# Moving weight loads behind output transposes in a fused attention and feed-forward kernel on Trainium2

## The chip, the cores and the metric

The kernel runs on one core of one Trainium2 chip. The metric is the device time of one execution in microseconds (us), as the median over several executions. In the profile, PE is TensorE (PEld its weight loads), DVE is VectorE, ACT is ScalarE, POOL is GpSimd and SP is SyncE. A q behind an engine's name means an instruction of its sequencer, such as one that issues a DMA. SP does no arithmetic here: it only issues DMAs and waits, strictly one after another.

## The reference

One transformer block with conditioning is computed for 2048 rows of width 1024, all in bf16:

```
mod = (silu(c) @ w_mod) in six rows:  sa, ca, ga, sb, cb, gb
h = layernorm(x) * (1 + ca) + sa
q = h @ wq                               # 32 heads of 128
k, v = the last 512 rows of the caches   # 4 key/value heads, each used by 8 query heads
o = softmax(q k^T / sqrt(128)) v
x = x + ga * (o @ wo)
h = layernorm(x) * (1 + cb) + sb
x = x + gb * ((silu(h @ w_gate) * (h @ w_up)) @ w_down)   # inner width 3584
```

## The kernel before, in words

**Tiling.** The rows are cut into 4 chunks of 512. One long loop (line 895) runs over `i`, one head of one chunk per iteration: 32 heads by 4 chunks are 128 heads. The loop is a software pipeline. In iteration `i` PE first projects the queries of head `i+3` (`qproj`: 8 matmuls of 512 columns, weights from a `wq` tile), then multiplies queries and keys of head `i-1` (`scores`: 4 matmuls of 512 columns, with the exponentials on ACT), then multiplies probabilities and values of head `i-2` (`pv`: 16 matmuls of 129 columns). After that DVE divides by the row sums (L824, L827), and SP issues a DMA transpose of the head's output into `oT_all` (L830). When the last head of a chunk is through `pv`, `oproj` multiplies all 32 turned heads by `wo`: 8 pieces of 32 matmuls, in the order of the heads. The last chunk's `oproj` is written out by hand behind the loop (lines 1005 to 1014), so that 44 matmuls on heads 0 to 27 come before the first that need heads 28 to 31. Then comes the feed-forward part, 28 tiles (`gateup`) and 8 pieces (`down`) for each chunk.

**Loads.** The query weights come in groups of four heads, 1 MB each (`load_wq`, L357), into slots that are used in turn. One is issued in every iteration with `i % 4 == 1`, for heads that `qproj` reaches four iterations later. Between iterations 34 and 85, 24 blocks of `w_mod` are loaded through a DMA transpose (`load_mt`, L582); these are the "turned weights", and DVE reduces each one four iterations after its load (`mod_col`, L587). The output weights `wo` (L840) and parts of x (L302) are loaded during the first iterations, and `ln_task` puts in DMA transposes for the next chunk's layer norm (L448). All of these are issued by SP in program order. The gate and up weights (`load_wgu`, L998 and L1000) are issued by ACT; the first two groups, four loads of 1 MB, stand directly behind the loop.

**Order.** Nothing is scheduled automatically. Each engine runs its instructions in the order in which the program emits them, and a small tracker puts in a wait where a buffer (`_Buf`) is read after a write, or written after a read. What the tracker knows of a buffer is its name, not its bytes: two pieces of one tile that share a `_Buf` wait for each other.

**The end.** `down` writes each finished piece with two DVE instructions of `resid` (L846 multiplies, L848 adds the residual and writes the tile `y_s`), and SP sends it to DRAM. The last 128 rows go out in three pieces of 512, 384 and 128 columns (L1071), from one tile `y_s[3]` under one `_Buf`, `B_y[3]`.

Of the kernel before, what the change touches and what calls it, by code (L numbers as in the profile page):

```python
# [7 lines left out]
P = 128  # L8
# [122 lines left out]
def bass_adaLN_cond__sliding_block_cached__swiglu_ffn__prompt_kernel(  # L131
# [17 lines left out]
    Hq = HD // Dh  # L149
# [111 lines left out]
    with nc.Block() as block:  # L261

        @block.gpsimd
        def _(g):
# [23 lines left out]
            def finish(gen):  # L288
                while gen in bg:
# [6 lines left out]
                 reads=[B_ident], writes=[B_ident])  # L296
# [50 lines left out]
            def wq_slot(gidx):  # L347
                return gidx if gidx <= NWQ else (gidx + 1) % NWQ
# [3 lines left out]
            def load_wq(gidx):  # L352
                if gidx >= NCH * HG:
                    return
                sl = wq_slot(gidx)
                hg = gidx % HG
                T.op(Q_wq[sl], lambda: SP.dma_start(  # L357
                    wq_s[sl], A_wq[:, hg * 512:(hg + 1) * 512].rearrange("(k p) n -> p k n", p=P)), writes=B_wq[sl])
# [139 lines left out]
            def mod_ca(hf, k):  # L498
# [6 lines left out]
                 reads=[B_cT, B_ident], writes=[PB[XB]])  # L505
# [7 lines left out]
                 reads=[B_x[tl]], writes=[B_ns4[tl], B_acc])  # L513
# [10 lines left out]
            def norm_last(c0, n):  # L524
# [9 lines left out]
                 reads=[B_acc], writes=[B_nm])  # L534
            T.op(ACT, lambda: A.activation(nsc4[tl], x_res[:, tl, :], AF.Square, bias=nmean[:, 0:1], accum_out=acc[:, 1:2]),
                 reads=[B_x[tl], B_nm], writes=[B_ns4[tl], B_acc])
# [41 lines left out]
            def load_mt(n):  # L578
                if n < 2:
                    for b_ in B_qT[NQT:]:  # L580
                        B_mt[n].absorb(b_)
                T.op(Q_mt[n % 2], lambda: SP.dma_start_transpose(  # L582
                    mt[n % 2].rearrange("p (a b) -> p a b", a=1), w_mod[:, (NF + n) * P:(NF + n + 1) * P]),
                     writes=[B_mt[n % 2]])
# [34 lines left out]
            B_oT = [_Buf("oT%d" % h) for h in range(Hq)]  # L619
# [224 lines left out]
            def resid(b, t, c0, n, ri, k, dst, dst_buf):  # L844
                s = k % 2
                T.op(DVE, lambda: V.tensor_tensor(tmp[s][:, 0:n], bank(b, n), rowb[ri][:, c0:c0 + n], ALU.mult),  # L846
                     reads=[B_row[ri]], writes=[PB[b], B_tmp[s]])
                T.op(DVE, lambda: V.tensor_tensor(dst[:, c0:c0 + n], tmp[s][:, 0:n], x_res[:, t, c0:c0 + n], ALU.add),  # L848
                     reads=[B_tmp[s], B_x[t]], writes=[dst_buf])
# [43 lines left out]
            LOADT = {Hq + 2 + (9 * n) // 4: n for n in range(NL)}  # L893
            LOADO = {5 + (21 * p) // 8: p for p in range(8)}
            for i in range(1, NA + 2):
                ch, h = divmod(i, Hq)
                if i % 4 == 1 and i > 5 or i == 4:
                    load_wq((i + 4) // 4 + 1)
                if 2 <= i < NQ0:
                    q_shifted(i)  # L900
                if i in (2, 3):
                    load_wga(i - 2)
                if i in LOADX:
                    load_x(LOADX[i])
                if i in LOADO:
                    load_wo(LOADO[i])
                if i in GATET:
                    gate_turn(GATET[i])
                if i in GATES:
                    gate_sum(GATES[i])  # L910
                if i in TURNT:
                    if i > Hq:
                        T.op(DVE, lambda: V.tensor_copy(mstg[:, 0:DT], mcol[:, 2 * DT:3 * DT]), reads=[B_mcol], writes=[B_mstg])
                    row_turn()
                if i in PUTT:
                    row_put(*PUTT[i])
                if i in GETT:
                    row_get(*GETT[i])
                if i == 7:
                    add_ln1(1)  # L920
                if h == 2 and 1 <= ch < NCH - 1:
                    add_ln1(ch + 1)
                if h == 2 and ch == NCH - 1:
                    add_ln2(0)
                if i + LEAD < NA:
                    if (i + LEAD) % Hq == 0:
                        finish(ln1[(i + LEAD) // Hq])
                    if i == 1:
                        scores(0)
                    if i in (1, 3, 5):  # L930
                        q_bias_mm(i + 1, i + 3, XB)
                    if i > NQ0:
                        qproj(i + LEAD)
                    elif i % 2 == 1:
                        qproj_mm(NQ0 + i // 2, QB, 0, HK)
                    else:
                        qproj(NQ0 - 1 + i // 2, QB, HK)
                if i - 4 in LOADT:
                    n = LOADT[i - 4]
                    mod_col(n)  # L940
                    g0, last = divmod(n, DT)
                    if last == DT - 1:
                        mod_take(g0, B_late[g0 + 1])
                        if g0 == 1:
                            mod_gain(1, B_late[2], B_g[1])
                if i in LOADT:
                    load_mt(LOADT[i])
                n = i - (NA - LEAD)
                if 0 <= n <= 2:
                    oproj_mm(NCH - 1, 0, QB, 8 * n, 8 * n + 8)  # L950
                elif n >= 3:
                    oproj_mm(NCH - 1, 1, XB, 8 * (n - 3), 8 * (n - 3) + 8)
                if 1 <= i - 1 < NA:
                    scores(i - 1)
                for gk in {2: (1,), 4: (2,), 6: (3,)}.get(i, ()):
                    k_turn(gk, XB)
                    kd, ks = k_evac(gk, XB)
                    T.op(DVE, lambda: V.tensor_copy(kd, ks), writes=[PB[XB], B_kT[gk]])
                    if gk == Hkv - 1:
                        for b_ in B_hT[1]:  # L960
                            for kb in B_kn:
                                b_.absorb(kb)
                if 0 <= i - 2 < NA:
                    pv(i - 2)
                    ch2, h2 = divmod(i - 2, Hq)
                    if h2 == Hq - 1 and ch2 < NCH - 1:
                        oproj(ch2)
                run_bg(1)
                for n in GATEP.get(i, ()):
                    gate_part(n)  # L970
                if i in GATER:
                    gate_row(GATER[i])
                if i == max(GATER):
                    gate_split()
# [10 lines left out]
            B_wg = [_Buf("wg%d" % i) for i in range(NWG)]  # L985
            B_wu = [_Buf("wu%d" % i) for i in range(NWG)]
            wg_s = [arena.at(OFF_G[i], [DT, 512], BF16, [B_wg[i]]) for i in range(2)]
# [2 lines left out]
            Q_wu = [dq("q_wu%d" % i, A) for i in range(NWG)]  # L990
            FG = FT // 4

            def load_wgu(G):
                if G >= NCH * FG:
                    return
                fg = G % FG
                sl = G % NWG
                T.op(Q_wg[sl], lambda: A.dma_start(  # L998
                    wg_s[sl], B_w_gate[:, fg * 512:(fg + 1) * 512].rearrange("(k p) n -> p k n", p=P)), writes=[B_wg[sl]])
                T.op(Q_wu[sl], lambda: A.dma_start(  # L1000
                    wu_s[sl], B_w_up[:, fg * 512:(fg + 1) * 512].rearrange("(k p) n -> p k n", p=P)), writes=[B_wu[sl]])

            load_wgu(0)
            load_wgu(1)
            HL = Hq - 4
            oproj_mm(NCH - 1, 1, XB, 16, HL)
# [16 lines left out]
            B_sg = [_Buf("sg%d" % i) for i in range(2)]  # L1023
            sg_s = [arena.at(OFF_SG + i * KB, [CH], BF16, [B_sg[i]]) for i in range(2)]
            B_y = [_Buf("y%d" % i) for i in range(4)]
            y_s = [arena.at(OFF_Y + i * 2 * KB, [D], BF16, [B_y[i]]) for i in range(4)]
            NWDP = 7
            B_wd = [_Buf("wd%d" % i) for i in range(NWDP)]
# [28 lines left out]
            def down(ch):  # L1057
                last = ch == NCH - 1
                pieces = [(j, hf * 512, 512) for j in range(TPC) for hf in range(2)]
                if last:  # L1060
                    pieces[-1:] = [(TPC - 1, 512, 384), (TPC - 1, 896, 128)]
                for k, (j, c0, n) in enumerate(pieces):
                    t = ch * TPC + j
                    b = 4 + k % 2
                    for ft in range(FT):
                        mm(bank(b, n), guT[:, ft, j * P:(j + 1) * P], wd_s[:, ft, c0:c0 + n],
                           ft == 0, ft == FT - 1, [B_wd[ft // (FT // NWDP)], B_gu[ft]], PB[b])
                    resid(b, t, c0, n, 1, k, y_s[t % 4], B_y[t % 4])
                    q = t % 4
                    if last and j == TPC - 1:  # L1070
                        T.op(Q_fin[k % 3], lambda: SP.dma_start(of[t * P:(t + 1) * P, c0:c0 + n], y_s[q][:, c0:c0 + n]),  # L1071
                             reads=[B_y[q]])
                    elif c0 == 512:
                        T.op(Q_out[q], lambda: SP.dma_start(of[t * P:(t + 1) * P, :], y_s[q]), reads=[B_y[q]])
                    run_bg(1)
# [48 lines left out]
```

## Time and profile before

| what | us |
|---|---|
| median of 3 runs | 1272.57 (1272.42 to 1273.69) |
| profiled execution, its own time | 1273.07 |
| its span, first to last instruction | 1271.1 |
| PE busy | 1264.0 (99%) |
| DVE busy | 485.8 (38%) |
| ACT busy | 341.6 (27%) |
| POOL busy | 55.9 (4%) |
| DMA queue of SP, share of the 16 DMA engines | 32.3% |
| DMA queue of ACT, share of the 16 DMA engines | 14.7% |

The first three rows say how the numbers stand to each other: the profiled execution took 2.0 us outside its span, and was itself 0.5 us above the median. The busy times are shares of the span; PE is busy almost throughout, at a granted clock of 1.00, and the other engines work beside it. The shares of the queues are averages over parts with very different loads.

### The profile page before, as it was taken

How to read it: one execution, taken by the hardware profiler on the slowest of the kernel's cores; microseconds unless marked ns; L12 is line 12 of the kernel's file. 1: busy time of each engine (PE TensorE's matmuls, PEld its weight loads, DVE VectorE, ACT ScalarE, POOL GpSimd, SP SyncE). 2: the span in 40 equal slices, each digit the busy share in tenths (PEclk: the TensorE clock that was granted, in tenths of full speed). 3: DMA queues.
4: the chain of work that ended last, by engine and by line, in shares of the span. 5: the costliest groups of instructions: out<-in, count | busy, mean ns of one | idle time of the engine just before them, and what ended most of it. 6: DMA issues, size and time to landing. Idle time of an engine off the chain costs nothing.

```text
span 1271.1 us, 17772 instructions
## 1 busy us (share of the span) xinstructions
PE 1264.0 (99%) x7595; PEld 641.9 (50%) x7595; DVE 485.8 (38%) x897; ACT 341.6 (27%) x389; POOL 55.9 (4%) x95
## 2 busy tenths in 40 slices
PE   9999999999999999999999999999999999999998
PEld 5655545555455554555544444444444444444444
DVE  4676226764257641365322321233212321221122
ACT  4655204553035550155510111011100111011100
POOL 1530000000000000000000000000000000000000
PEclk9999999999999999999999999999999999999999
DMA  9999405975028550066252973055512654044200
GB/s 314 283 257 218 91 1 117 206 147 121 1 62 175 129 136 16 9 133 142 38 145 100 290 240 100 25 157 150 166 42 72 176 141 133 17 132 150 67 9 25
DMA packets 238765, 156.67 MB, mean 123 GB/s; under 512 B 131680, under 2 KB 224608, under 8 KB 238688
## 3 DMA queue, kind: packets, MB, share of 16 engines
q1 hardware_dynamic: 180432, 96.83, 32.3%
q10 hardware_dynamic: 58256, 58.73, 14.7%
q8 instruction: 59, 0.97, 0.3%
q14 instruction: 18, 0.15, 0.0%
HBM read 120.33 MB, written 4.20 MB: 98 GB/s over the span
## 4 chain that ended last, share of the span: by engine, by line
PE 97%; DMA 2%; DVE 0%; SPq 0%; issue 0%; DVEq 0%
PE ps L271 97%; DMA arena<-arena 1%; DMA arena<-in_w_mod_dram 0%; PE ps L275 0%; SPq L309 0%; DMA out_dram<-arena 0%; DVE arena L827 0%; SPq L334 0%; DVE arena L587 0%; DVE arena L848 0%; DVE arena L490 0%; DVE arena L638 0%; DVE tmp L846 0%; SPq L582 0%; DVE rl L824 0%
## 5 line engine op out<-in xcount | busy, mean ns | idle before, releaser
L271 PE MATMUL ps<-arena 128*128 128x512 bf16 (+1 forms) x7354 | 1258.3, 334 | 3.5 <-POOL arena L298 2.0
L271 PEld LDWEIGHTS ps<-arena 128*128 128x128 bf16 x7354 | 633.4, 98 | 621.2 <-issue 2.2
L806 ACT ACTIVATE arena<-ps 128x1024 bf16<-128x1024 f32 x256 | 261.9, 1023 | 346.5 <-PE ps L271 334.8
L1053 ACT ACTIVATE arena<-ps 128x512 bf16<-128x512 f32 x112 | 66.9, 597 | 506.9 <-PE ps L271 506.9
L1054 DVE TENSOR_TENSOR arena<-ps,arena 128x512 bf16<-128x512 f32 x112 | 77.4, 691 | 276.3 <-PE ps L271 276.3
L846 DVE TENSOR_TENSOR tmp<-ps,rowb 128x512 f32<-128x512 f32 (+1 forms) x65 | 44.4, 683 | 319.9 <-PE ps L271 319.9
L638 DVE CAST arena<-ps 128x512 bf16<-128x512 f32 x120 | 82.8, 690 | 48.5 <-PE ps L271 48.5
L827 DVE TENSOR_TENSOR arena<-ps,rl 128x512 bf16<-128x512 f32 x128 | 88.5, 691 | 4.7 <-DVE rl L824 0.2
L824 DVE RECIPROCAL rl<-ps 128x4 f32<-128x4 f32 x128 | 23.3, 182 | 112.8 <-PE ps L271 112.8
L423 POOL TENSOR_SCALAR rstd<-mv 128x1 f32<-128x1 f32 x28 | 6.1, 216 | 912.5 <-DVE mv L422 912.5
L418 DVE BATCH_NORM_STATS2 st<-x_res 128x6 f32<-128x512 bf16 x62 | 42.3, 683 | 3.6 <-DMA x_res<-in_A_x_dram 3.5
L587 DVE SCALAR_TENSOR_TENSOR arena<-arena 128x1024 bf16<-128x1024 bf16 x24 | 29.1, 1214 | 0.0
L848 DVE TENSOR_TENSOR arena<-tmp,x_res 128x512 bf16<-128x512 f32 (+2 forms) x33 | 22.3, 676 | 2.1 <-DMA out_dram<-arena 1.0
L848 DVE TENSOR_TENSOR x_res<-tmp,x_res 128x512 bf16<-128x512 f32 x32 | 22.1, 692 | 1.1
L434 DVE TENSOR_SCALAR arena<-arena,gain,mod_bf 128x512 bf16<-128x512 bf16 x56 | 21.2, 420 | 0.0
L429 DVE TENSOR_SCALAR nsc<-x_res,mv,rstd 128x1024 bf16<-128x1024 bf16 x30 | 19.2, 641 | 0.0
L425 POOL TENSOR_TENSOR rstd<-rstd,mhalf 128x1 f32<-128x1 f32 x28 | 15.7, 559 | 2.3
L765 POOL TENSOR_SCALAR arena<-arena,sc_bf 128x512 f32<-128x512 bf16 x8 | 12.6, 1576 | 0.5 <-POOL arena L767 0.2
L767 POOL TENSOR_TENSOR arena<-arena 128x512 f32<-128x512 f32 x8 | 10.1, 1265 | 0.7
L422 DVE BATCH_NORM_AGGREGATE mv<-st 128x2 f32<-128x12 f32 x28 | 5.8, 209 | 1.0
L271 PEld LDWEIGHTS ps<-sc_bf,arena 128*128 128x128 bf16 x128 | 4.4, 96 | 1.8 <-DMA arena<-in_w_mod_dram 0.4
L271 PE MATMUL ps<-sc_bf,arena 128*128 128x1 bf16 x128 | 4.6, 164 | 0.2
(57 smaller groups left out, 62.6 us busy)
## 6 DMA issues: line engine op xcount, KB each, us to landing
arena<-in_A_wq_dram SPq DMA_DIRECT2D x31, 1024.0 KB, 5.9
arena<-in_B_w_gate_dram ACTq DMA_DIRECT2D x28, 1024.0 KB, 5.3
arena<-in_B_w_up_dram ACTq DMA_DIRECT2D x28, 1024.0 KB, 7.9
arena<-in_A_wo_dram SPq DMA_DIRECT2D x8, 1024.0 KB, 7.1
arena<-in_B_w_down_dram SPq DMA_DIRECT2D x7, 1024.0 KB, 8.0
out_dram<-arena SPq DMA_DIRECT2D x15, 256.0 KB, 2.0
x_res<-in_A_x_dram SPq DMA_DIRECT2D x3, 1024.0 KB, 6.7
arena<-arena SPq DMA_TRANSPOSE x132, 2.8
```

The lines of the kernel that those rows point to most:

```text
L271: T.op(PE, lambda: TE.matmul(out_ap, lhsT, rhs, start=start, stop=stop, skip_group_check=skip), reads=reads, writes=[bank_buf])
L418: T.op(DVE, lambda: V.bn_stats(st_[sl][:, hf * 6:hf * 6 + 6], x_res[:, t, hf * 512:hf * 512 + 512]), reads=[B_x[t]], writes=[B_st[sl]])
L434: T.op(DVE, lambda: V.tensor_scalar(dst[:, dt, :], dst[:, dt, :], gain[gi][:, dt:dt + 1], mod_bf[:, ccol + dt:ccol + dt + 1], op0=ALU.mult ...
L587: T.op(DVE, lambda: V.scalar_tensor_tensor(mt[n % 2], mt[n % 2], 1.0, sc_row, op0=ALU.mult, op1=ALU.mult, accum_out=mcol[:, n:n + 1]), rea ...
L638: T.op(DVE, lambda: V.tensor_copy(qT_s[qs], bank(b)), writes=[PB[b], B_qT[qs]])
L806: T.op(ACT, lambda: A.activation(ex_s[es][:, 2 * kp:2 * kp + 2, :], banks2(SCB + 2 * kp), AF.Exp, scale=att_scale), writes=[PB[SCB + 2 * k ...
L824: T.op(DVE, lambda: V.reciprocal(rl[r][:, :].rearrange("p (a b) -> p a b", a=2), psap(PVB * 512 + P, [[512, 2], [130, 2]])), writes=both + ...
L827: T.op(DVE, lambda: V.tensor_tensor(o_s[os_].rearrange("p (a b) d -> p a b d", a=2), psap(PVB * 512, [[512, 2], [130, 2], [1, P]]), rlb, A ...
L846: T.op(DVE, lambda: V.tensor_tensor(tmp[s][:, 0:n], bank(b, n), rowb[ri][:, c0:c0 + n], ALU.mult), reads=[B_row[ri]], writes=[PB[b], B_tmp ...
L848: T.op(DVE, lambda: V.tensor_tensor(dst[:, c0:c0 + n], tmp[s][:, 0:n], x_res[:, t, c0:c0 + n], ALU.add), reads=[B_tmp[s], B_x[t]], writes= ...
L1053: T.op(ACT, lambda: A.activation(sg_s[ss], bank(gb), AF.Silu), writes=[PB[gb], B_sg[ss]])
L1054: T.op(DVE, lambda: V.tensor_tensor(guT[:, ft, :], bank(ub), sg_s[ss], ALU.mult), reads=[B_sg[ss]], writes=[PB[ub], B_gu[ft]])
```

## The change

Three edits are made.

1. In the loop, `load_wq` (for all but iteration 4) and `load_mt` are emitted behind `pv(i - 2)`, and so behind the output transpose of head `i-2`, but before `oproj` where a chunk ends. They stood ahead of it: `load_wq` at the start of the iteration, `load_mt` after `qproj` and `mod_col`.
2. The first gate load behind the loop gets the turned outputs of heads 30 and 31 (`B_oT[30]`, `B_oT[31]`) as buffers that it reads. ACT therefore waits for those two transposes to land before it issues this load and the three behind it.
3. The last piece of the output, 128 columns, gets a buffer of its own, `B_yl`, in place of `B_y[3]`. The bytes stay where they were.

```
             for i in range(1, NA + 2):
                 ch, h = divmod(i, Hq)
-                if i % 4 == 1 and i > 5 or i == 4:
+                if i == 4:
                     load_wq((i + 4) // 4 + 1)
...
-                if i in LOADT:
-                    load_mt(LOADT[i])
...
                 if 0 <= i - 2 < NA:
                     pv(i - 2)
                     ch2, h2 = divmod(i - 2, Hq)
+                    if i % 4 == 1 and i > 5:
+                        load_wq((i + 4) // 4 + 1)
+                    if i in LOADT:
+                        load_mt(LOADT[i])
                     if h2 == Hq - 1 and ch2 < NCH - 1:
                         oproj(ch2)
...
-            def load_wgu(G):
+            def load_wgu(G, after=()):
...
                 T.op(Q_wg[sl], lambda: A.dma_start(
-                    wg_s[sl], B_w_gate[:, fg * 512:(fg + 1) * 512].rearrange("(k p) n -> p k n", p=P)), writes=[B_wg[sl]])
+                    wg_s[sl], B_w_gate[:, fg * 512:(fg + 1) * 512].rearrange("(k p) n -> p k n", p=P)),
+                     reads=list(after), writes=[B_wg[sl]])
...
-            load_wgu(0)
+            load_wgu(0, B_oT[Hq - 2:])
             load_wgu(1)
...
+            B_yl = _Buf("yl")
...
-                    resid(b, t, c0, n, 1, k, y_s[t % 4], B_y[t % 4])
                     q = t % 4
+                    yb = B_yl if last and k == len(pieces) - 1 else B_y[q]
+                    resid(b, t, c0, n, 1, k, y_s[q], yb)
                     if last and j == TPC - 1:
                         T.op(Q_fin[k % 3], lambda: SP.dma_start(of[t * P:(t + 1) * P, c0:c0 + n], y_s[q][:, c0:c0 + n]),
-                             reads=[B_y[q]])
+                             reads=[yb])
```

## The prediction

> **What bounds the kernel now.** I read the page first, then the waits, the chain that ended last, the timeline at the places that these name, and the groups by shape. From the page, busy time (share of the span, instructions) and the clock granted in the 40 slices:
>
> ```profile
> PE 1264.0 (99%) x7595; PEld 641.9 (50%) x7595; DVE 485.8 (38%) x897; ACT 341.6 (27%) x389; POOL 55.9 (4%) x95
> PEclk9999999999999999999999999999999999999999
> ```
>
> PE is idle for 1271.1 - 1264.0 = 7.1 us, and its clock is full throughout. No matmul is added or removed, so only these 7.1 us, and stalls that matmul records hide by overlapping, can change. The waits (us in total, times, longest) tell what they are:
>
> ```profile
> PE ps L271 <- POOL arena L298: 2.0, 1, 2.0
> PEld ps L271 <- DMA arena<-arena: 1.9, 3, 1.0
> DVE arena L848 <- DMA out_dram<-arena: 1.0, 1, 1.0
> PE ps L271 <- DMA arena<-arena: 0.7, 2, 0.5
> ```
>
> The first is the start, which the change leaves alone. The second and fourth are matmuls, and their weight loads, that wait for output transposes; the third is the last DVE instruction, behind a DMA. The chain that ended last (start, us, what) gives their places:
>
> ```profile
> 307.25 0.47 SPq L582
> ...
> 307.82 5.64 DMA arena<-arena
> ...
> 641.39 9.35 DMA arena<-arena
> ...
> 1266.73 0.57 DVE arena L848
> ...
> 1267.32 1.62 DMA out_dram<-arena
> ...
> 1269.04 0.29 DVE arena L848
> ```
>
> The timeline shows both PE stalls, and what SP did ahead of the first:
>
> ```profile
> 305.06 0.53 SPq L357 DMA_DIRECT2D arena<-in_A_wq_dram  x1
> 306.43 1.30 SPq L582 DMA_TRANSPOSE arena<-in_w_mod_dram  x1
> 307.82 1.48 SPq L830 DMA_TRANSPOSE arena<-arena  x1
> ...
> 313.51 2.76 PE L271 MATMUL ps<-arena 128*128 128x512 bf16 x12 [0.52 <-DMA arena<-arena]
> ...
> 650.79 19.38 PE L271 MATMUL ps<-arena 128*128 128x512 bf16 x89 [0.23 <-DMA arena<-arena]
> ```
>
> At 307.82 the transpose of a chunk's last head goes out behind a 1 MB load and a turned load, and `oproj` stops for it.
>
> **How long the stalls are.** The brackets count from the modelled end of the matmul before. Matmuls start every (19.38 - 0.38) / 88 = 0.216 us, but one lasts 0.379 us by the groups by shape; so a bracket leaves out 0.379 - 0.216 = 0.16 us. The stalls are 0.52 + 0.16 = 0.68 us and 0.23 + 0.16 = 0.39 us. Bounds are the brackets alone (0.75 together) and PEld's idle time at the same places (1.01 and 0.72).
>
> **Edit 1, what it gains.** DVE's L827 of that head ends at 307.25 in the chain, so the transpose can be issued there. Transposes land 2.4 us after issue at best and 2.7 in the median (min/median/max of L830: 2.4/2.7/9.8), here by 310.0; PE wants it at 313.51 - 0.68 = 312.8. That stall goes, 0.68 us. At the other two chunk ends inside the loop PE has no gap, only PEld one of 0.17 us, so nothing is gained there. Late next is nothing: the two loads that now follow serve heads behind 55 us of `oproj`.
>
> **Edit 1, what it costs.** The 28 query loads from iteration 9 on move behind one more output transpose each, and with it behind DVE's L827 of that head. In a quiet stretch (SP's rows, then DVE's cast of the first head that uses this load):
>
> ```profile
> 570.11 0.53 SPq L357 DMA_DIRECT2D arena<-in_A_wq_dram  x1
> 572.32 1.19 SPq L830 DMA_TRANSPOSE arena<-arena  x1
> ...
> 583.60 0.69 DVE L638 CAST arena<-ps 128x512 bf16<-128x512 f32 x1 [0.82 <-PE ps L271]
> ```
>
> The landing of all L357 loads, from the line's own view:
>
> ```profile
> DMA to landing us min/median/max: 5.4/5.9/10.6
> ```
>
> The load goes out at 572.32 + 1.19 = 573.5, 3.4 us later. PE starts on it 8 x 0.216 + 0.2 us ahead of the cast, at 581.7. So 8.2 us are left for a landing of 5.9: 2.3 to spare, no stall. The tight places are in the first chunk, where `wo` and x share the queue. The load at 95.96 took 9.2 us, to 105.2, and is wanted at 107.5 (cast at 109.40). Moved, it lands between 0.5 us later (in a full queue it only changes places with a small transpose) and 3.4 later: from 1.8 to spare to 1.1 late. The load at 70.13 took 7.5, to 77.6, wanted at 79.5 (cast at 81.43); the next transpose was issued 0.6 us behind it, so its shift is 1.2 (one transpose's issue) to 2.8: from 0.7 to spare to 0.9 late. After these the worst landing is 7.2 us at 543.49, which keeps 0.9. So edit 1's cost is 0 to 2.0 us. I take 0: the queue holds the same work in another order, which is the first end of each pair.
>
> [...]
>
> The 24 turned loads go out about 3.4 us later too. The shortest time from such an issue to the DVE reduction that reads it (L587) is 231.7 - 219.6 = 12.1 us, the longest landing 6.7, so 2.0 are left. The first one, at 141.36, is now queued behind the next chunk's first transpose (198.88), lands by 206.8 at the latest, and is read at 210.8. If one were late, DVE would hold up its cast and so PE. L448, L840 and L302 are queued on SP behind the moved instructions as before, only up to 3 us later; none has a waiter that near.
>
> **Edit 2.** The last two transposes were issued at 638.76 and 641.39 and took 9.8 and 9.3 us, while four 1 MB loads from ACT (637.62 to 640.26) were in flight; without these, by 2.4 to 2.7 us, they land by 644.1. PE wants them at 650.4: the stall of 0.39 goes. Behind ACT's new wait are the four loads, a table load of 1.28 us, and then nothing until the first L1053 at 689.20. The loads landed 17.5 us after the first issue (640.26 + 14.8); from 644.1 that is 661.6, and PE wants the first at 689.20 - 16 x 0.216 = 685.7. With 24 us of cover the wait costs nothing.
>
> **Edit 3.** The last L848 could start when its L846 ends, 1267.70 + 0.29 = 1267.99, and starts at 1269.04. With its own buffer it starts at 1268.02, a gain of 1.02. The final DMA then goes out at about 1268.34 with the piece before still in flight; its landing of 1.4 us may become 1.7 as for the first of the three pieces. So the gain is 0.7 to 1.0; I take 1.02, since DMAs of 96 and 32 KB leave the engines nearly empty.
>
> **The sum.** 0.68 + 0.39 + 1.02 = 2.09 us off the span: 1269.0. With the 2.0 us outside, the profiled execution would be 1271.0 against 1273.07. That execution lies 0.5 above the median, so the median becomes 1272.57 - 2.09 = 1270.5 us. A measurement of this kernel can tell about 0.2% from no change, 2.55 us; the forecast, 0.16%, is inside that.
>
> **Rivals.**
> *Only the end is gained (0.13).* The stalls hang on how DMAs fall, and the profiled execution is 0.5 us above the median; ordinary runs may have less of them. The third edit alone gives 1272.57 - 1.02 = 1271.5. It includes the case that the last two DMAs get in each other's way, and that one or two query loads are late (1272.57 - 2.09 + 2.0 = 1272.5).
> *Longer stalls than shown (0.18).* The slowest of the three runs is 1.1 us above the median, so some runs hold more than this profile. By PEld's idle times the gain is 1.01 + 0.72 + 1.04 = 2.77: 1269.8, faster by more than 0.2%. Against it: the matmul starts show 1.07 for the two, and the median run is the shorter one.
> *Query weights arrive late (0.07), slower.* The place is `qproj` at the start of every fourth iteration. It decides from a landing of 8.2 us, which the profile shows passed only at the start and in the crowded first chunk; to pass +0.2% it must cost 2.09 + 2.55 = 4.64 us, 0.17 us for each of 28 loads. At a mean landing of 8.5 us it would be 28 x 0.3 = 8.4 us: 1278.9. Against it: the median is 5.9.
> That an edit does not take hold I give nothing: the order of emission is the order of execution.
>
> The forecast itself has 0.62. Chances: faster 0.18, same 0.62 + 0.13 = 0.75, slower 0.07. The range runs from the second rival's 1269.8 less 0.3 for the scatter of medians to the late loads' 1272.5 plus 0.3: 1269.5 to 1272.8.
>
> **What would show it.** In the profile after: no PE wait for `arena<-arena` at the second chunk's end or behind the loop; the chunk-end transpose ahead of L357 on SP, landing in under 3 us; ACT's four loads issued after 644; the last L848 within 0.1 us of its L846. A PE or PEld wait for `in_A_wq_dram` inside the loop, above all near 79 and 107 us, would prove the third rival. A span outside 1268 to 1270 us would say that a term is mis-sized.

## Result, and the profile after

| | before | after |
|---|---|---|
| median, us (22 runs each) | 1272.94 | 1270.87 |
| span of the profiled execution, us | 1271.1 | 1268.8 |

The ratio is 0.9984, 95% interval 0.9978 to 0.9991: 2.07 us less by the medians, where 2.09 was forecast. The forecast of 1270.5 lies 0.4 us below the measured time because before's median is 1272.94 over 22 runs, not 1272.57 as over the first three.

The page after, first line of busy times:

```profile
PE 1255.6 (99%) x7454; PEld 641.9 (51%) x7595; DVE 486.3 (38%) x897; ACT 341.7 (27%) x389; POOL 56.2 (4%) x95
```

Its matmuls are 141 fewer than before's 7595, while the weight loads are all there: the records are missing, not the work. PE's busy time of this profile is therefore not comparable, and I read the stalls from other engines' rows. SP's timeline at the end of the second chunk:

```profile
303.44 4.69 SPq L830 DMA_TRANSPOSE arena<-arena  x2
308.22 0.53 SPq L357 DMA_DIRECT2D arena<-in_A_wq_dram  x1
308.81 2.09 SPq L582 DMA_TRANSPOSE arena<-in_w_mod_dram  x1
```

The two transposes now stand ahead of both loads; the second, of the chunk's last head, goes out at 306.94 and lands 2.5 us later, where it took 5.6. ACT's first load behind the loop, in the timelines before and after:

```profile
637.62 0.40 ACTq L998 DMA_DIRECT2D arena<-in_B_w_gate_dram  x1
```

```profile
642.91 0.41 ACTq L1000 DMA_DIRECT2D arena<-in_B_w_gate_dram  x1
```

After the change it comes 0.06 us after the last transpose landed (640.37 + 2.48 = 642.85). The prediction's sign was an issue after 644; the loop itself ended 1.02 us earlier than before (its last transpose went out at 640.37 in place of 641.39), so the order is as forecast. The end, in the timeline:

```profile
1265.89 1.36 SPq L1076 DMA_DIRECT2D out_dram<-arena  x2
1266.28 0.29 DVE L846 TENSOR_TENSOR tmp<-ps,rowb 128x128 f32<-128x128 f32 x1 [0.41 <-PE ps L271]
1266.61 0.29 DVE L848 TENSOR_TENSOR arena<-tmp,x_res 128x128 bf16<-128x128 f32 x1
```

L848 follows its L846 after 0.04 us, and the last DMA is issued at 1266.93, 1.04 us behind the one before it. Of the waits, no row names `arena<-arena` or `out_dram<-arena` any more. One PE wait for query weights is left, 0.7 us; it stands at 11.46 us, at the start and ahead of every load that was moved.

**Where the time went, by stage.** Five instructions mark stages: DVE's first cast (L638, head 8), its casts for heads 64 and 72, ACT's first Silu (L1053, later L1057), and the landing of the last output DMA. Their times are 32.69, 290.58, 374.50, 689.20 and 1270.80 us before, and 32.35, 290.25, 373.47, 687.78 and 1268.37 after. The differences, with those of the experiments below, formed in the same way:

| profile | to the first cast | to head 64 | second `oproj` (64 to 72) | to the first Silu | to the last landing |
|---|---|---|---|---|---|
| before | 32.69 | 257.89 | 83.92 | 314.70 | 581.60 |
| after | 32.35 | 257.90 | 83.22 | 314.31 | 580.59 |
| edit 1 alone | 32.40 | 258.21 | 83.23 | 315.33 | 581.60 |
| edit 1 alone, again | 32.46 | 257.90 | 83.23 | 314.55 | 581.59 |
| edit 2 alone | 32.46 | 257.90 | 83.94 | 314.31 | 581.59 |
| edit 3 alone | 32.69 | 257.90 | 83.89 | 314.51 | 580.60 |
| edits 2 and 3 | 32.53 | 257.90 | 83.83 | 314.31 | 580.59 |
| query loads of edit 1 alone | 32.32 | 258.63 | 83.23 | 314.67 | 581.59 |
| turned loads of edit 1 alone | 32.58 | 257.90 | 83.22 | 315.33 | 581.60 |
| chunk ends alone, with 2 and 3 | 32.39 | 257.90 | 83.22 | 314.31 | 580.59 |
| changed, again | 33.00 | 257.93 | 83.23 | 314.31 | 580.59 |

After against before: 0.70, 0.39 and 1.01 us less in the last three columns, 2.10 together. The first column, the start, differs by up to 0.65 us between two profiles of the same kernel (32.35 and 33.00), so I put its difference down to scatter.

### The profile page after: what moved, and what is told of

It reads as the page before. It is cut to its first block, busy times and chain, and to the rows that moved or that the text cites. A ratio compares the mean times of both kernels' runs of the same rounds, so it can differ in the third digit from the quotient of the medians.

```text
span 1268.8 us, 17632 instructions
## 1 busy us (share of the span) xinstructions
PE 1255.6 (99%) x7454; PEld 641.9 (51%) x7595; DVE 486.3 (38%) x897; ACT 341.7 (27%) x389; POOL 56.2 (4%) x95
## 4 chain that ended last, share of the span: by engine, by line
PE 98%; issue 1%; DMA 1%; SPq 0%; DVE 0%
PE ps L271 98%; DMA arena<-in_A_wq_dram 1%; SPq L334 0%; SPq L309 0%; PE ps L275 0%; DVE tmp L846 0%; DVE arena L848 0%
## 5 line engine op out<-in xcount | busy, mean ns | idle before, releaser
L1057 ACT ACTIVATE arena<-ps 128x512 bf16<-128x512 f32 x112 | 66.9, 597 | 499.9 <-PE ps L271 499.9
L846 DVE TENSOR_TENSOR tmp<-ps,rowb 128x512 f32<-128x512 f32 (+1 forms) x65 | 44.4, 683 | 318.8 <-PE ps L271 318.8
L638 DVE CAST arena<-ps 128x512 bf16<-128x512 f32 x120 | 82.9, 690 | 48.4 <-PE ps L271 48.4
L848 DVE TENSOR_TENSOR arena<-tmp,x_res 128x512 bf16<-128x512 f32 (+2 forms) x33 | 22.3, 676 | 1.1
L848 DVE TENSOR_TENSOR x_res<-tmp,x_res 128x512 bf16<-128x512 f32 x32 | 22.1, 692 | 1.1
```

Source lines behind the costliest of these rows:

```text
L638: T.op(DVE, lambda: V.tensor_copy(qT_s[qs], bank(b)), writes=[PB[b], B_qT[qs]])
L1057: T.op(ACT, lambda: A.activation(sg_s[ss], bank(gb), AF.Silu), writes=[PB[gb], B_sg[ss]])
```

## Experiments

My theory: each edit removes one wait, the three waits are in series on PE and at the end, and the gains add. The rivals were late query weights, and gains given back at a later wait.

**One edit at a time.** Edit 1 alone is the first block of the diff above; edit 2 alone is this, with the new parameter of `load_wgu` from the diff, on the kernel before:

```
...
-            load_wgu(0)
+            load_wgu(0, B_oT[Hq - 2:])
```

and edit 3 alone puts `B_yl` in place of `B_y[3]` for the last piece. What was expected of each:

> Edit 1 alone: the query loads and the turned loads behind the output transpose, the rest as before. My theory (the three edits remove three separate waits, and the sum is exact): in the profile the gap at the second chunk's oproj (0.68 us) is gone, the gap behind the loop (0.39 us) and the wait of the last L848 for the DMA (about 1.0 us) are still there, so 0.7 us less than before (ratio 0.9995), which timing alone can hardly tell from 1. Rival (query weights arrive late): PE or PEld waits for the query weights in the loop, and the time is above before's by the sum of these waits. Rival (the gain of the loop is given back later, at the end of the loop where transposes stand behind the loads of ACT): the gap behind the loop grows from 0.39 to about 1.1 us and the time is that of before.

> Edit 2 alone: ACT's first gate load waits for the transposes of heads 30 and 31. My theory: the last two transposes land 2.4 to 4 us after issue in place of 9.8 and 9.3, the gap behind the loop (0.39 us) is gone, the gap at the second chunk's oproj (0.68) and the wait of the last L848 stay: 0.4 us less than before (0.9997). Rival (ACT's wait delays the gate and up weights): the first feed-forward tile starts later against the last oproj piece, and PE waits for in_B_w_gate or in_B_w_up; the time is then above before's.

> Edit 3 alone: the last piece of 128 columns has a buffer of its own. My theory: the last L848 starts within 0.1 us of its L846's end in place of 1.04 us behind it, the last DMA is issued 1.0 us earlier, and lands in 1.4 to 1.7 us: 1.0 us less than before (0.9992); both PE gaps stay. Rival (the last DMA, now in flight beside the one before it, is slowed by it): its landing grows from 1.4 us to as much as 2.4, and the time is that of before.

The ratios to before are 0.9998 (0.9990 to 1.0007), 0.9993 (0.9984 to 1.0002) and 0.9990 (0.9982 to 0.9999). Only the third interval leaves out 1, so the profiles must decide. Edit 2 alone, its waits:

```profile
PEld ps L271 <- DMA arena<-arena: 1.0, 1, 1.0
DVE arena L848 <- DMA out_dram<-arena: 1.0, 1, 1.0
PE ps L271 <- DMA arena<-arena: 0.5, 1, 0.5
```

The stall at the second `oproj` and the wait at the end are still there; the stall behind the loop is gone (314.31 against 314.70 in the table), and the last transpose lands 2.48 us after issue. Edit 3 alone takes 1.00 us off the last column and leaves the other stalls; its last DMA, in flight beside the one before it, lands in 1.45 us, so the rival of a slower landing falls. Edit 1 alone, its waits:

```profile
PEld ps L271 <- DMA arena<-arena: 1.3, 1, 1.3
...
PE ps L271 <- DMA arena<-arena: 0.9, 1, 0.9
PEld ps L271 <- DMA arena<-in_A_wq_dram: 0.8, 2, 0.6
```

Here both rivals that I had named came true. The gain at the second `oproj` is there (83.23), but behind the loop the stall grew from 0.39 to 1.02 us (315.33 - 314.31), and 0.3 us went ahead of head 64 (258.21), where PEld waits for query weights at 232.72. The span is 1271.1, as before. A second profile of the same kernel, on another chip:

> Edit 1 alone, a second look. In the first its gain at the second chunk's oproj was given back: 0.3 us at the query load for head 48, 0.6 us behind the loop, where the last transpose landed 0.6 us later against the loop's end than in the profile of before. My theory: the lateness for head 48 comes and goes between executions, between 0 and 0.8 us; the late landing behind the loop is scatter of a full queue and need not return. Rival: both return at the same size.

The span is 1270.1. Head 48's load is in time (257.90), and the stall behind the loop is 0.24 us (314.55). Neither cost returned at its size. The timed runs say the same: over the 11 of edit 1 alone the median span is 1270.4 us, over the 27 of before beside them 1270.9, so that edit 1 alone gains about 0.5 and its first profile is one of the longer runs. Without edit 2 the stall behind the loop was 0.20 to 1.02 us in the six profiles that have it with the full cover; why the landing in a queue full of ACT's loads varies by 0.8 us is open. With edit 2 this column is 314.31 in all six profiles of the table.

**Which load stood in the way at the second `oproj`.**

> Of edit 1 the query loads alone are moved, the turned loads stay ahead of the transpose. It asks which load the second chunk's last transpose stood behind. My theory (the 1 MB load ahead of it in the same queue delayed it, the turned load only by its issue of 0.5 us and 0.4 us of transport): the transpose lands within 3 to 4 us of its issue and PE's gap at that chunk end is gone, as with the whole edit. Rival (the turned load, also a transpose, is what holds it): the gap of 0.7 us stays.

> Of edit 1 the turned loads alone are moved, the query loads stay at the start of the iteration. My theory (a queue in order: the transpose lands about 0.5 us behind the 1 MB load ahead of it): issued at 307.3 it lands at 312.5 in place of 313.5, about when PE comes to it (312.8), so the gap falls from 0.7 to 0 to 0.3 us although the transpose still takes about 5 us. Rival (the turned load is what holds it): it lands in 2.4 to 2.7 us of its issue.

The stall is gone in both (83.23 and 83.22). With the query load moved, the transpose landed 2.5 us after issue. With only the turned load moved, in the view of L830 for that transpose:

```profile
DMA to landing us min/median/max: 5.2/5.2/5.2
```

It still queued behind the 1 MB load, and landed at 312.4, just ahead of PE. So the query load makes most of the delay, and the turned load the last microsecond, which became the stall: moving either is enough here, and moving the query loads gives the larger margin. But in its one profile the kernel with the query loads alone lost 0.7 us elsewhere. Its timeline at head 48:

```profile
233.06 1.41 PEld L271 LDWEIGHTS ps<-arena 128*128 128x128 bf16 x8 [0.74 <-DMA arena<-in_A_wq_dram]
233.29 1.46 PE L271 MATMUL ps<-arena 128*128 128x512 bf16 x6 [0.79 <-DMA arena<-in_A_wq_dram]
```

Its load went out at 225.57 and took 7.4 us, behind x's load for the fourth chunk (L302, at 219.10), a turned load and two output transposes. That load of x is issued in iteration 40, and not among the first ones as I had written of L302.

**How much lead the query loads need.** The changed kernel with each load one iteration later still:

```
-                    if i % 4 == 1 and i > 5:
-                        load_wq((i + 4) // 4 + 1)
+                    if i % 4 == 2 and i > 6:
+                        load_wq((i + 3) // 4 + 1)
```

> The changed kernel with each query load one iteration later still, behind the next output transpose (i % 4 == 2 in place of 1). It tests the spare time that I took for the moved loads (8.1 us from issue to need, 5.4 to 5.9 to land, 2.3 to spare). My theory: one more period of 3.5 us leaves 4.6 us for a landing of 5.4 to 5.9, so each of the 28 loads is 0.9 to 1.3 us late, the seven of the crowded first chunk up to 2.6, and PE or PEld waits for the query weights at each: 30 us more than the changed kernel in all (25 to 40), 1296 to 1311 us. [...] Rival (another cover hides the load, such as work of PE that runs ahead): less than 5 us more.

1318.6 us, ratio 1.0353 (1.0337 to 1.0368): 47.7 us above the changed kernel's 1270.87, or 47.0 when each is set against the kernel before as timed beside it (1318.6 - 1273.63 + 2.07). That is more than I had expected. The waits:

```profile
PEld ps L271 <- DMA arena<-in_A_wq_dram: 44.4, 29, 5.0
PE ps L271 <- DMA arena<-in_A_wq_dram: 38.8, 28, 4.9
```

All 28 loads are late. With the 0.16 us that a bracket leaves out, PE stops for 38.8 + 28 x 0.16 = 43.3 us: 19 stops are of 1.0 to 1.4 us, where 0.9 to 1.3 was expected of most, eight are of 1.9 to 2.3, and one is of 5.0. This profile's span is 1318.5 - 1268.8 = 49.7 us longer than the changed kernel's; the remaining 6.4 us go with the clock, which is 1.00 throughout in the changed kernel. The table by windows of this kernel (window, length, busy us and instructions of PE, PEld, DVE, ACT and POOL, granted clock, DMA share, GB/s) shows where it falls:

```profile
60.00:76.00 16.00, 11.12 (x68) 5.76 (x67) 6.12 (x10) 5.30 (x6) 6.56 (x7) 0.79 1.04 239
```

```profile
400.00:404.00 4.00, 4.00 (x23) 2.20 (x22) 1.83 (x3) 1.79 (x2) 0.00 (x0) 0.57 0.36 69
624.00:629.00 5.00, 3.67 (x10) 1.36 (x11) 0.48 (x2) 0.21 (x1) 0.00 (x0) 0.66 0.35 82
```

It is low around the longest stop, 5.0 us up to 70.22, and behind two of 2.1 us. The three rows lack 0.21 x 16 + 0.43 x 4 + 0.34 x 5 = 6.8 us of full clock, a part of it while PE stood still, which fits the 6.4. So the spare time that I took is right in kind: 3.4 us less lead cost nothing, another 3.5 us cost 47.7. Here lead had no price until the landing passed it.

**The transposes behind the loop, with little cover.** Both kernels keep all the work, but put the 28 matmuls of the third piece behind the first use of heads 28 to 31:

```
-            oproj_mm(NCH - 1, 2, SCB, 0, HL)
...
-                oproj_mm(NCH - 1, k, b, HL, Hq)
+                oproj_mm(NCH - 1, k, b, 0 if k == 2 else HL, Hq)
```

> Edits 1 and 3, without edit 2, and with the cover behind the loop cut: the 28 matmuls of the third oproj piece that stood ahead of the first use of heads 28 to 31 come after it, so 16 matmuls (3.5 us) in place of 44 (9.5 us) lie between the loop and that use. The work is the same. It makes the disputed delay of the last transposes large enough to time. My theory (the transposes are slow because ACT's four loads are in flight): they land 9 to 10 us after issue as before, PE stops for about 6.5 to 7 us, and the time is 1270.9 + 0.4 + 6.1 = 1277.4 us or more; a stop of this length may also lower PE's clock for a while, which I put at 0 to 2 us on top. Rival (the transposes at the end are slow by themselves): the same time here, but the partner with edit 2 is as slow.

> The changed kernel, all three edits, with the same cut of the cover behind the loop. My theory: the last two transposes land 2.4 to 4 us after issue, at about 642.9, where PE is there at about 642.9 too: a gap of 0 to 0.3 us, and 1270.9 to 1271.3 us in all. Rival (the transposes at the end are slow by themselves, not because of the loads): a stop of 6 us as in its partner, 1277 us.

Without edit 2 it took 1280.3 us, with it 1271.0: 1.0052 (1.0035 to 1.0068) and 0.9984 (0.9975 to 0.9993) of before. The view of L830 for the last two transposes, without edit 2 and then with it:

```profile
DMA to landing us min/median/max: 9.9/10.2/10.4
```

```profile
DMA to landing us min/median/max: 2.5/3.4/4.4
```

That settles the cause: the same transposes take two to four times as long (10.4 against 4.4 us, and 9.9 against 2.5) when ACT's loads are in flight, though SP and ACT have queues of their own. The stop, in the timeline without edit 2:

```profile
649.78 0.39 PE L271 MATMUL ps<-arena 128*128 128x512 bf16 x1 [4.92 <-DMA arena<-arena]
...
651.94 3.17 PE L271 MATMUL ps<-arena 128*128 128x512 bf16 x7 [1.78 <-DMA arena<-arena]
```

and its table by windows, columns as above:

```profile
630.00:640.00 10.00, 9.89 (x83) 6.04 (x83) 2.62 (x6) 6.15 (x6) 0.00 (x0) 1.00 0.25 49
640.00:650.00 10.00, 5.08 (x36) 2.58 (x34) 0.88 (x2) 1.28 (x1) 0.00 (x0) 1.00 1.13 250
650.00:660.00 10.00, 8.00 (x27) 3.18 (x28) 2.77 (x4) 0.00 (x0) 0.00 (x0) 0.66 0.61 187
```

The stage to the first Silu (698.81 - 375.06 = 323.75) is 9.4 us longer than the 314.31 of a kernel without the stop. The stop itself is 4.92 + 1.78 + 2 x 0.16 = 7.0 us; the other 2.4 us go with the reduced clock, 0.66 over the next 10 us (3.4 us of full clock, 1.0 of it in the second stop), somewhat above the 0 to 2 that I had allowed. With edit 2 this stage is 314.31 with the short cover too: 3.5 us of cover in place of 9.5 are enough.

**What edit 1 is worth beside the others, and a narrower one.** Edits 2 and 3 without edit 1; all three, but with loads moved only where a chunk ends; and the changed kernel as yardstick on the same chip. The narrower one, against the changed kernel:

```
-                if i == 4:
+                if i % 4 == 1 and i > 5 and h != 1 or i == 4:
...
+                if i in LOADT and h != 1:
+                    load_mt(LOADT[i])
...
-                    if i % 4 == 1 and i > 5:
+                    if h == 1 and i > 5:
...
-                    if i in LOADT:
+                    if i in LOADT and h == 1:
```

> Edits 2 and 3, without edit 1: what edit 1 is worth beside the others. My theory: the gap behind the loop and the wait of the last L848 are gone, the gap of 0.7 us at the second chunk's oproj stays, no query load is late: 1.4 us less than before, 0.7 more than the changed kernel (0.9989 of before). Rival (edit 1 costs what it gains, because a query load for head 48 is late in some executions, as the profiles of edit 1 alone and of its query loads alone showed): the same time as the changed kernel or less.

> The changed kernel, but with the loads behind the output transpose in the three iterations that end a chunk alone (33, 65, 97); in all others query and turned loads stand where they stood before. My theory: the gap at the second chunk's oproj is gone as with the whole edit 1, since only there does PE wait for a transpose, and the query loads keep the lead they had before (9.4 to 11.6 us from issue to need, at least 1.9 to spare): the same span as the changed kernel's profile, and a median of 0 to 0.3 us less. Rival (moving all loads gains something else as well): it stays above the changed kernel by more than 0.3 us.

> The changed kernel unaltered, on the chip of the two others, as their yardstick: 0.9984 of before, spare of the query load for head 48 between -0.8 and 0.6 us.

The ratios to before are 0.9987 (0.9979 to 0.9996), 0.9986 (0.9977 to 0.9995) and 0.9983 (0.9973 to 0.9992); the medians 1271.73, 1271.39 and 1271.00 us. By the stages edit 1 is worth 0.61 us here (83.83 against 83.22). In edits 2 and 3 alone the only stall left in the loop, by the timeline, is:

```profile
313.27 1.90 PE L271 MATMUL ps<-arena 128*128 128x512 bf16 x8 [0.44 <-DMA arena<-arena]
```

The narrower kernel reaches the same stages as the changed one to the hundredth, and its query loads have at least 2.8 us to spare in the loop, where the changed one had 0.4 to 0.6 at head 28 and at head 48. Its timed runs are not better (1271.39 against 1271.00, inside both intervals): no gain is shown, only the margin.

## Why the prediction was right or wrong

- **The size of the stalls.** 0.68, 0.39 and 1.02 were predicted; 0.70, 0.39 and 1.01 came. Adding to a bracket what overlapping matmuls hide (0.16 us) was right; the brackets alone would have given 0.75 for the first two, PEld's idle times 1.73. That the 0.39 of one profile stood for the ordinary run was in part luck: without edit 2 this stall is 0.20 to 1.02 us from profile to profile.
- **Edit 1's gain.** Right: the transpose lands at 309.4, PE stops no longer.
- **Edit 1's cost, taken as 0 of a range to 2.0.** Right for the changed kernel, in both its profiles, but with luck. The two tight places that I named kept 1.1 us (head 20: landed 78.07, wanted 79.17) and 0.5 us (head 28: landed 106.60, wanted 107.14). But one step was wrong: "After these the worst landing is 7.2 us at 543.49, which keeps 0.9." I had looked for the longest landing where the shortest spare time counts. The load at 222.89, for head 48, landed in 7.0 us with 2.8 to spare before; moved, it goes out 7.6 us ahead of its use (224.82 to 232.38), not the 8.2 taken for every load, and keeps 0.4 (landed 231.95), and was late by 0.3 and 0.7 us in two of the seven profiles that have all query loads moved by one place. So the third rival's mechanism is real at one place, at 0.3 to 0.7 us where it needed 4.64.
- **The third rival's price.** 0.3 us for each of 28 loads was worked out for a landing just over the lead. One iteration later still, the loads cost 1.8 us each in the profile (49.7 / 28): 43.3 of the 49.7 us in stops, and the rest by the clock, which the price left out.
- **Edit 2.** Right, and the cover of 24 us was ample: the Silu of the first tile follows the loop at the same distance (314.31 us in the table) in every kernel that has the edit.
- **Edit 3.** Right at the upper end of 0.7 to 1.0: the last landing takes 1.44 us as before.
- **The second rival, longer stalls than shown.** Its price did not come: by PEld's idle times 2.77 us would have gone. But its ground, that some runs hold more than the profile shows, has something in it. Timed beside each other, the spans of before go from 1270.2 to 1272.8 us (27 runs), those of edit 2 alone from 1270.4 to 1271.0 (11 runs), and those of edit 3 alone, which keeps the stall behind the loop, from 1269.4 to 1272.0 (11 runs). So the wait that edit 2 removes seems to make most of the scatter within the span; no long case was profiled, so this is not shown directly. The rest sits at the start and outside the span: over all profiles but that of the loads made later still the first cast falls between 32.15 and 33.94 us, and the time outside the span between 1.8 (1270.63 - 1268.8, after) and 3.0 us (1274.05 - 1271.1, edit 1 alone).
- **The first rival, only the end is gained.** It fell too, though its reason was sound: the stall behind the loop does vary, 0.20 to 1.02 us.
- **The price of lead.** The runs show 0 us for the first 3.4 us of lead given up (in the quiet stretch from 581.7 - 570.11 = 11.6 us to 581.7 - 573.5 = 8.2) and 47.7 for the next 3.5.

## What to carry to other kernels

When PE is busy throughout, look for the few waits in the profile that are in series with it, and size each from start to start, since modelled ends hide part of a gap (0.16 us here). Here the gains of three separate waits, sized so, added up to 2.10 us by stages where 2.09 was forecast; a wait on a crowded queue can still vary from run to run (0.20 to 1.02 us). A small transfer that PE waits for soon should be issued ahead of large ones that nobody needs soon, in its own queue and in any other queue whose loads are in flight with it: here an output transpose landed in 2.5 us in place of 5.6 behind a 1 MB load and a turned load of its own queue, and in 2.5 to 4.4 in place of 9.9 to 10.4 beside four of ACT's. Before moving a load, list the spare time (wanted minus landed) of every instance, not the landing times, and move only those where something is gained.

## What the runs showed of the hardware

- A stop of PE of 7.0 us (two parts, 5.1 and 1.9) was followed by a granted clock of 0.66 over 10 us and cost 2.4 us more than itself; in the 16 us that hold the stop of 5.0 us, up to 70.22, the clock was 0.79; stops of 0.4 to 0.7 us left it at 1.00. With the loads made late, two stops of 2.1 us (1.98 and 1.96 in brackets, at 398.89 and 625.33) were followed by 0.57 (400 to 404 us) and 0.66 (624 to 629), while five others of the same length were not: the mean over that profile is 0.995, which lacks 0.005 x 1318.5 = 6.6 us, and the three rows above hold 6.8. The low clock was short: 1.00 again from 404 to 408 us, and 0.69 from 624 to 628, 0.89 from 628 to 632 and 1.00 from 632 to 656. So stops of 2.1 us lowered the clock in two cases of seven; what sets these two apart is not shown.
- The clock was low at the start of one profile: without edit 2 and with little cover it was 0.66 from 11 to 16 us, 1.00 in before's, and the first cast came at 33.94 in place of 32.69.
- A DMA transpose of one head lands 2.4 to 2.5 us after issue at best, 5.0 to 5.6 us behind a 1 MB load of its own queue at the chunk ends, and 9.2 to 10.5 us beside four such loads from ACT's queue. In the profiles of before, after and the narrower kernel, 54 transposes had no DMA beside them but others of their own kind, and each took 2.4 to 2.5; 13 had a 16 KB packet of the instruction queue in flight as well (q8 in the DMA view) and took 2.4 to 4.4. Head 126's, issued at 637.73 in after, is one of these: 4.1 us.
- The two pairs of profiles of one program agree to 0.03 us in every stage behind the first cast that has no late DMA. The scatter between executions is at the start, in late DMAs, and outside the span.
